# A recurrent attention layer and a gated MLP in one program: the preparation of the MLP's weights is spread differently over the end of the attention part

## The chip, the cores and the metric

One core of a Trainium2 chip runs the whole program. The metric is the device time of one execution in microseconds (us). Before the change three runs gave 663.85, 665.86 and 666.63 us, a median of 665.86 us.

## The reference, cut to what matters

Two parts follow each other. The first is a recurrence over 768 tokens for 4 x 8 pairs of batch and head, each with a state of 40 x 40:

```
for t in range(S):                                   # S = 768
    y[t]  = r[t] @ state
    Sa    = state @ a[t]
    state = state * w[t] - outer(Sa, b[t]) + outer(v[t], k[t])
```

Its output, laid out as x (4 batches x 768 tokens x 320 features), goes through a gated MLP:

```
h = gelu(x @ w_in)                       # 320 -> 1024
u, v = h[..., :512], h[..., 512:]
v_n = layer_norm(v) * g_ln
v_s = w_sg @ v_n + b_sg                  # over the 768 tokens
out = x + (u * v_s) @ w_out              # 512 -> 320
```

"First layer" below is w_in, "last layer" is w_out.

## The kernel before, in words

**Attention.** The 768 tokens are cut into 12 chunks of 64. A chunk is worked off in two halves (`half`, line 488), and each half takes two of the four batches through a chain: `chain1` (PE writes ru, ACT copies it to rhsb), `chain_t` (a transpose of the state, copied to s), `chain2` (PE multiplies by the inverse xt, ACT writes vu), `chain3` (PE writes sp, DVE adds it to the state sc, ACT copies sc to vs; ut and vut), and, for the batches of the half before, `chain4` (PE writes pq, DVE masks it into pqs) and `chain5` (PE writes yp, DVE scales it into yt, SP stores yt to xd in DRAM). The inverse xt of a chunk comes out of a long run of small steps, most of them on GpSimd (tg, x), and then of `inv_back`, `inv_g` and `inv_x` (x1z, gp, gs, xp, and ACT's copies into xt).

**MLP.** In front of its products the weights are prepared. They come as 64-bit floats, and `split64` (line 680) turns a piece into a high and a low 32-bit part in six steps: `load` (SP starts a DMA of the raw piece into a buffer stg), `size` (ACT: sc<-stg), `fields` (DVE: two operations on sc), `scale` (DVE: lt<-stg, stg<-stg,sc, sc<-stg), `parts` (ACT: lt<-lt, and the cast wih<-stg or woh<-stg), `low` (three operations on GpSimd, or on DVE for some pieces of the first layer: lt, stg, and wil or wol). The first layer has 12 pieces of 128 x 256 (`weights_in`), called k0 to k11 below; the last layer has four of 128 x 256 and four of 128 x 64 (`weights_out`), called o0 to o3 and s0 to s3. A raw large piece is 256 KB. The buffers stg are a ring of three (`stage`, line 658) that all pieces share in the order in which they are loaded, so a load waits until the piece three loads back has gone through `low`.

**What sets the order.** Every instruction keeps program order on its engine (`InOrder`, line 105), and SP starts all DMAs of this part of the program in one order. The order is written as numbers: a chunk is 28 positions long, a half 14, and chunk c begins at 28c. `side` (line 886) lists the steps of every weight piece with a position, `half` sorts them among the chain's steps, whose positions are in CH, and calls them in turn. For a first-layer piece `DEC` gives the position of `fields` and whether `low` is on DVE (0) or GpSimd (1), and `DSTEP` the distances of the six steps from it; `DECO` and `DSTEPO` do the same for the last layer, whose `low` is always on GpSimd. So a load is a place in SP's queue, and `size` is a place in ACT's queue; neither knows of the other but by the transfer that `size` waits for.

In SP's queue a half ends with four stores of yt (xd<-yt), two loads of rt and one of vut (`load_rv`), and the next begins with a load of vs; at position 294 there is also `load_x`, four loads of xt from xd. Once the attention part is over, positions go on with `in_v` (three products hv at 338, 342 and 345.87) and the last two batches' chain4 and chain5, then the MLP's main loop (`run`) follows.

Of the kernel before, what the change touches and what calls it, by code (L numbers as in the profile page):

```python
# [53 lines left out]
G1 = 0.044715  # L54
ENDS = {(9, 1): (("g", 0.01),), (10, 1): (("r", 0.01),), (11, 0): (("i", 5.0),)}
PIN = 266.02
DSTEP = ((-9.0, -1.0, 0.0, 0.7, 1.4, 2.4), (-9.0, -1.0, 0.0, 0.7, 1.4, 3.0))
DEC = ((275.0, 0), (280.0, 0), (285.0, 0), (289.66, 0), (295.0, 1), (300.0, 0), (305.0, 1), (310.0, 1), (315.0, 1),
    (320.0, 1), (325.0, 1), (330.0, 1))
PX = 294.02  # L60
# [9 lines left out]
REST = 8  # L70
SGS = (5, 3, 5, 6, 7, 8, 8, 11, 10, 11, 12, 11)
PO = 313.2
DECO = (332.0, 334.0, 336.0, 338.5, 340.5, 342.5, 344.5, 347.0)
DSTEPO = (-4.0, -1.0, 0.0, 0.7, 1.4, 2.4)
SGE = "GVGVGVGVVVGG"
SECOND = 14.0
# [535 lines left out]
class Mlp:  # L612
# [273 lines left out]
    def side(self, c, hf):  # L886

        def at(p, f):
            plan.append((p, f))

        plan = []
        if self.plan is None:
# [4 lines left out]
            def step(k, i):  # L897
                if i == 0:
                    steps[k] = self.weights_in()[k](self.G if DEC[k][1] else self.V)
                steps[k][i]()  # L900

            for k in range(12):
                for i, d in enumerate(DSTEP[DEC[k][1]]):
                    at(max(PIN + 0.1, DEC[k][0] + d), lambda k=k, i=i: step(k, i))
# [7 lines left out]

            for k, p in enumerate(DECO):
                for i, d in enumerate(DSTEPO):
# [171 lines left out]
```

## Time and profile before

| | |
|---|---|
| median of three runs | 665.86 us |
| the profiled execution | 665.51 us, of which its span is 663.8 us |
| PE / DVE / ACT / POOL busy | 87% / 77% / 59% / 58% of the span |
| mean granted TensorE clock | 0.90 of full speed |
| chain that ended last | PE 50%, DVE 24%, ACT 14%, issue 7%, DMA 3% |
| stretch of the weight pieces' `size` on ACT | 326.2 to 415.6 us from the span's start |
| PE busy in the slices of 16.6 us from 398 us and from 431 us | 2 and 6 tenths |

How to read it: a profile row gives the start in us from the span's start, the duration, the engine, the operation, the tile written and the tiles read, a count where rows were merged, and in square brackets how long the engine had been idle and what ended that. SPq rows are DMAs being started, not moved: the row says when SP was busy with the start. The 1.7 us between the span and the execution's time lie outside of the span.

### The profile page before, as it was taken

How to read it: one execution, taken by the hardware profiler on the slowest of the kernel's cores; microseconds unless marked ns; L12 is line 12 of the kernel's file. 1: busy time of each engine (PE TensorE's matmuls, PEld its weight loads, DVE VectorE, ACT ScalarE, POOL GpSimd, SP SyncE). 2: the span in 40 equal slices, each digit the busy share in tenths (PEclk: the TensorE clock that was granted, in tenths of full speed). 3: DMA queues.
4: the chain of work that ended last, by engine and by line, in shares of the span. 5: the costliest groups of instructions: out<-in, count | busy, mean ns of one | idle time of the engine just before them, and what ended most of it. 6: DMA issues, size and time to landing. Idle time of an engine off the chain costs nothing.

```text
span 663.8 us, 22411 instructions
## 1 busy us (share of the span) xinstructions
PE 580.4 (87%) x8950; PEld 525.7 (79%) x8950; DVE 510.4 (77%) x1097; ACT 391.8 (59%) x1106; POOL 385.9 (58%) x869
## 2 busy tenths in 40 slices
PE   6547998989999899998978692969999999999996
PEld 5436787878888778887967682859999999999995
DVE  7875778989889898898777569788679668667732
ACT  5555687978878788797763744654245335424410
POOL 6588886787877878778782455464332433333321
PEclk8555599999999999999978676789999999999999
DMA  6722233443443433433344332331002002100001
GB/s 223 235 78 78 81 95 104 114 118 102 115 109 107 121 106 108 108 93 101 81 113 119 90 88 73 93 110 47 31 13 91 12 19 68 35 31 1 31 24 41
DMA packets 57617, 56.54 MB, mean 85 GB/s; under 512 B 35936, under 2 KB 47456, under 8 KB 57504
## 3 DMA queue, kind: packets, MB, share of 16 engines
q1 hardware_dynamic: 57504, 55.02, 28.9%
q8 instruction: 72, 1.18, 0.7%
q14 instruction: 41, 0.34, 0.2%
HBM read 47.14 MB, written 7.86 MB: 83 GB/s over the span
## 4 chain that ended last, share of the span: by engine, by line
PE 50%; DVE 24%; ACT 14%; issue 7%; DMA 3%; POOL 1%; SPq 1%; DVEq 0%; POOLq 0%; ACTq 0%
PE sg L115 14%; PE op L115 7%; PE hu L115 5%; PE hv L115 5%; PE ab L115 4%; DVE at L115 3%; PE pq L115 3%; DVE fixed L115 3%; PE sp L115 2%; PE ru L115 2%; ACT nts L115 2%; DVE ex L115 2%; ACT xt L115 2%; PE yp L115 2%; DVE kb L115 2%
## 5 line engine op out<-in xcount | busy, mean ns | idle before, releaser
L115 POOL TENSOR_TENSOR tg<-x,n 128x126 f32<-128x126 f32 (+21 forms) x348 | 127.9, 368 | 45.6 <-DVE n L115 7.2
L115 POOL TENSOR_TENSOR x<-x,tg 128x126 f32<-128x126 f32 (+21 forms) x348 | 133.4, 383 | 27.3
L115 POOL TENSOR_TENSOR gx<-g,gy 128x384 fp32r<-128x384 f32 x32 | 33.4, 1046 | 84.6 <-ACT gy L115 83.5
L115 PE MATMUL ab<-at,kb 64*64 64x64 f32 x1536 | 44.5, 248 | 30.6 <-DVE kb L115 17.2
L115 PE MATMUL sg<-wsh,vh 128*128 128x384 f32 x192 | 65.4, 340 | 4.3 <-ACT vh L115 4.3
L115 ACT ACTIVATE nts<-ab 32x256 f32<-32x256 f32 x192 | 62.0, 323 | 10.4 <-DVE at L115 8.0
L115 PEld LDWEIGHTS ab<-at,kb 64*64 64x64 f32 x1536 | 35.9, 155 | 40.4 <-ACT junk L115 14.0
L115 PE MATMUL sg<-wsh,vl 128*128 128x384 f32 x192 | 65.5, 341 | 1.9 <-POOL vl L115 1.9
L115 PE MATMUL sg<-wsl,vh 128*128 128x384 f32 x192 | 65.1, 339 | 0.0
L115 PE MATMUL pq<-rt,vut 128*128 128x128 f32 x384 | 60.5, 306 | 3.8 <-ACT vut L115 3.0
L115 PE MATMUL yp<-pqs,kbt 128*64 128x64 f32 x768 | 50.2, 236 | 14.6 <-DVE pqs L115 13.1
L115 ACT CAST gy<-g 128x384 fp32r<-128x384 f32 x32 | 16.4, 514 | 74.5 <-DVE g L115 74.5
L115 PEld LDWEIGHTS pq<-rt,vut 128*128 128x128 f32 x384 | 52.3, 211 | 7.0 <-ACT vut L115 3.1
L115 PEld LDWEIGHTS yp<-pqs,kbt 128*64 128x64 f32 x768 | 40.7, 147 | 18.0 <-DVE pqs L115 13.7
L115 ACT COPY vs<-sc 64x160 f32<-64x160 f32 x88 | 28.3, 321 | 38.6 <-DVE sc L115 37.7
L115 ACT CAST vh<-v 128x512 fp32r<-128x512 f32 x24 | 14.9, 621 | 55.2 <-DVE v L115 55.2
L115 PE MATMUL yp<-rt,s 80*40 80x64 f32 x704 | 46.4, 232 | 0.0
L115 DVE SCALAR_TENSOR_TENSOR g<-sg,gl,bt 128x384 f32<-128x384 f32 x32 | 19.7, 616 | 32.2 <-PE sg L115 28.4
L115 POOL TENSOR_TENSOR vl<-v,vh 128x512 fp32r<-128x512 f32 x24 | 31.3, 1305 | 22.7 <-ACT vh L115 22.7
L115 DVE TENSOR_TENSOR at<-ab,mask 64x256 f32<-64x256 f32 x96 | 35.9, 409 | 7.6 <-PE ab L115 7.3
L115 PE MATMUL ru<-rhsb,xt 64*64 64x40 f32 x768 | 32.3, 242 | 9.9 <-ACT xt L115 9.9
L115 POOL TENSOR_TENSOR rs<-rs,mhalf 128x1 f32<-128x1 f32 x24 | 13.4, 560 | 46.8 <-DVE rs L115 41.8
(135 smaller groups left out, 1658.9 us busy)
## 6 DMA issues: line engine op xcount, KB each, us to landing
main<-main SPq DMA_DIRECT2D x88, 160.8 KB
vu<-vs SPq DMA_DIRECT2D x24, 160.0 KB
vs<-vb SPq DMA_DIRECT2D x24, 160.0 KB
rt<-rt SPq DMA_DIRECT2D x48, 80.0 KB
vut<-vt SPq DMA_DIRECT2D x24, 160.0 KB
xd<-yt SPq DMA_DIRECT2D x96, 40.0 KB
xt<-xd SPq DMA_DIRECT2D x16, 192.0 KB
out<-y SPq DMA_DIRECT2D x16, 192.0 KB
```

The lines of the kernel that those rows point to most:

```text
L115: return self.tc.keep_in_program_order(f(*a, **k))
```

## The change

Two tables of numbers change. The first-layer pieces' loads stand four positions ahead of `fields` in place of nine; everything else of these pieces keeps its position. The four large pieces of the last layer move from 332 to 338.5 to the gaps of the first layer's last four pieces, and the four small pieces are set 4 and 3 positions apart.

```
-DSTEP = ((-9.0, -1.0, 0.0, 0.7, 1.4, 2.4), (-9.0, -1.0, 0.0, 0.7, 1.4, 3.0))
+DSTEP = ((-4.0, -1.0, 0.0, 0.7, 1.4, 2.4), (-4.0, -1.0, 0.0, 0.7, 1.4, 3.0))
 DEC = ((275.0, 0), (280.0, 0), (285.0, 0), (289.66, 0), (295.0, 1), (300.0, 0), (305.0, 1), (310.0, 1), (315.0, 1),
     (320.0, 1), (325.0, 1), (330.0, 1))
...
-DECO = (332.0, 334.0, 336.0, 338.5, 340.5, 342.5, 344.5, 347.0)
+DECO = (317.5, 322.5, 327.5, 332.5, 336.0, 340.0, 344.0, 347.0)
 DSTEPO = (-4.0, -1.0, 0.0, 0.7, 1.4, 2.4)
```

The first place is SP's queue around position 268, in chunk 9. Before, k0 (stg_6819) stands a half ahead of the others; k1 (stg_6844) and k2 (stg_6892) follow the vs load:

```order
L115 DMA vs0_113<-vb 64x640
L115 DMA stg_6819<-w_in 128x512
L115 DMA vu0_131<-vs 64x640
L115 DMA xd_60<-yt_6682 40x4x64 x2
L115 DMA xd_60<-yt_6790 40x4x64 x2
L115 DMA rt1_125<-rt 40x2x256 x2
L115 DMA vut1_130<-vt 80x8x64
L115 DMA vs1_114<-vb 64x640
L115 DMA stg_6844<-w_in 128x512
L115 DMA stg_6892<-w2 128x512
```

Now, in the same place:

```order
L115 DMA vs0_113<-vb 64x640
L115 DMA vu0_131<-vs 64x640
L115 DMA xd_60<-yt_6682 40x4x64 x2
L115 DMA xd_60<-yt_6790 40x4x64 x2
L115 DMA rt1_125<-rt 40x2x256 x2
L115 DMA vut1_130<-vt 80x8x64
L115 DMA vs1_114<-vb 64x640
L115 DMA stg_6842<-w_in 128x512
L115 DMA stg_6890<-w_in 128x512
```

k0 is now stg_6842 and stands behind the stores, rt, vut and vs, where k1 stood; k1 (stg_6890) takes the place of k2. k2 itself moves to the place that k3 had, behind the next half's vut load.

The second place is SP's queue around position 294, with the loads of xt. Before, k5 (stg_7177) had been loaded ahead of these, and k6 (stg_7290) and k7 (stg_7337) follow the vs load:

```order
L115 DMA stg_7126<-w_in 128x512
L115 DMA stg_7177<-w2 128x512
L115 DMA vu0_131<-vs 64x640
L115 DMA xd_60<-yt_7221 40x4x64 x2
L115 DMA xd_60<-yt_7242 40x4x64 x2
L115 DMA rt1_125<-rt 40x2x256 x2
L115 DMA vut1_130<-vt 80x8x64
L115 DMA xt0_7265<-xd_60 128x384 x2
L115 DMA xt0_7265<-xd_60 64x384 x2
L115 DMA vs1_114<-vb 64x640
L115 DMA stg_7290<-w_in 128x512
L115 DMA stg_7337<-w_in 128x512
```

Now the two loads ahead are those of k3 (stg_7120) and k4 (stg_7175):

```order
L115 DMA stg_7120<-w_in 128x512
L115 DMA stg_7175<-w_in 128x512
L115 DMA vu0_131<-vs 64x640
L115 DMA xd_60<-yt_7219 40x4x64 x2
L115 DMA xd_60<-yt_7240 40x4x64 x2
L115 DMA rt1_125<-rt 40x2x256 x2
L115 DMA vut1_130<-vt 80x8x64
L115 DMA xt0_7263<-xd_60 128x384 x2
L115 DMA xt0_7263<-xd_60 64x384 x2
L115 DMA vs1_114<-vb 64x640
L115 DMA stg_7288<-w2 128x512
L115 DMA stg_7335<-w_in 128x512
```

k5 (stg_7288) has moved behind the stores, rt, vut, the four xt loads and vs, into the place that k6 had; k6 (stg_7335) is right behind it.

The third place is ACT's queue in the last chunk, from position 314 on. Before, k8 (stg_7466), k9 (stg_7526) and k10 (stg_7622) follow each other among the chain's copies:

```order
L115 ACTIVATE sc_7604<-stg_7466 128x256
L115 ACTIVATE vu0_131<-ru_7510 64x2x80 x2
L115 COPY vut0_129<-ut_7624 80x4x64
L115 ACTIVATE lt_7608<-lt_7608 128x256
L115 CAST wih_6815<-stg_7466 128x256
L115 CAST xh_7267<-xt0_7265 128x384 x3
L115 ACTIVATE sc_7648<-stg_7526 128x256
L115 COPY vut0_129<-ut_7652 80x4x64
L115 ACTIVATE lt_7658<-lt_7658 128x256
L115 CAST wih_6815<-stg_7526 128x256
```

Now:

```order
L115 CAST wih_6815<-stg_7524 128x256
L115 ACTIVATE sc_7632<-stg_7602 128x256
L115 ACTIVATE lt_7639<-lt_7639 128x256
L115 CAST woh_7590<-stg_7602 128x256
L115 CAST xh_7265<-xt0_7263 128x384 x3
L115 ACTIVATE sc_7660<-stg_7622 128x256
L115 COPY vut0_129<-ut_7667 80x4x64
L115 ACTIVATE lt_7673<-lt_7673 128x256
L115 CAST wih_6815<-stg_7622 128x256
L115 ACTIVATE sc_7702<-stg_7643 128x256
```

Between k8 (stg_7524) and k9 (stg_7622) stand the three ACT steps of o0 (stg_7602), and o1 (stg_7643) follows k9; DVE and GpSimd have the same pattern. PE's order is the same as before throughout.

## The prediction

> **What bounds the kernel now.** The time by stretches comes first: busy time of each engine, the granted PE clock, the DMA share and GB/s.
>
> ```profile
> 320.00:340.00 20.00, 16.03 (x441) 14.59 (x440) 15.85 (x35) 14.03 (x40) 16.24 (x44) 1.00 0.43 114
> 340.00:350.00 10.00, 9.76 (x131) 8.77 (x128) 8.08 (x21) 4.32 (x12) 8.48 (x20) 0.50 0.31 93
> 360.00:370.00 10.00, 5.32 (x162) 4.71 (x158) 4.08 (x13) 5.93 (x16) 1.22 (x2) 1.00 0.47 126
> 370.00:380.00 10.00, 6.96 (x76) 6.20 (x78) 5.89 (x14) 6.95 (x21) 5.46 (x8) 0.54 0.30 86
> 380.00:390.00 10.00, 10.00 (x126) 9.54 (x122) 4.83 (x15) 4.21 (x13) 3.99 (x6) 0.50 0.37 103
> 400.00:410.00 10.00, 2.83 (x40) 2.41 (x38) 8.87 (x21) 4.53 (x13) 5.57 (x8) 0.74 0.28 81
> 410.00:420.00 10.00, 4.32 (x40) 4.16 (x40) 9.37 (x27) 4.22 (x13) 6.64 (x16) 0.50 0.08 18
> ```
>
> No engine is the bound throughout. From 380 to 390 us PE is full, at half its clock, and DVE, ACT and POOL are idle for half of the time. From 400 to 420 us it is the other way round: PE works 7 us of 20 and DVE 18. Before that, from 360 to 380 us, nobody is busy: engines wait for each other. The waits of PE, by its timeline, say for whom:
>
> ```profile
> 339.03 0.31 PE L115 MATMUL ru<-rhsb,xt 64*64 64x40 f32 x2 [3.67 <-ACT xt L115]
> 372.87 0.43 PE L115 MATMUL ru<-rhsb,xt 64*64 64x40 f32 x2 [4.58 <-ACT xt L115]
> 405.44 0.48 PE L115 MATMUL yp<-pqs,kbt 128*64 128x64 f32 x4 [4.58 <-DVE pqs L115]
> 415.68 0.48 PE L115 MATMUL yp<-pqs,kbt 128*64 128x64 f32 x4 [8.27 <-DVE pqs L115]
> 417.59 1.33 PE L115 MATMUL hu<-xh,wih 128*128 128x384 f32 x3
> ```
>
> The first two wait for ACT's copies of the inverse, the next two for DVE's mask; hu is the first product that needs the first layer's other half. On ACT and DVE the weight pieces stand in the way: their steps are in the same queues, in fixed order. ACT's own timeline shows where k0, k2, k5 and k6 are sized:
>
> ```profile
> 326.06 0.29 ACT L115 COPY s<-tp 80x160 f32<-80x160 f32 x1
> 326.25 0.44 ACT L115 ACTIVATE sc<-stg 128x256 f32<-128x256 f32 x1
> 330.06 0.66 ACT L115 COPY vs<-sc 64x160 f32<-64x160 f32 x2 [3.09 <-DVE sc L115]
> 338.08 0.44 ACT L115 ACTIVATE sc<-stg 128x256 f32<-128x256 f32 x1
> 338.42 0.56 ACT L115 COPY xt<-xp 32x512 f32<-32x512 f32 x1
> 353.71 0.43 ACT L115 ACTIVATE sc<-stg 128x256 f32<-128x256 f32 x1
> 354.66 1.25 ACT L115 ACTIVATE vu<-ru 64x160 f32<-64x160 f32 x4 [0.52 <-PE ru L115]
> 358.58 0.28 ACT L115 COPY s<-tp 80x160 f32<-80x160 f32 x1
> 363.88 0.43 ACT L115 ACTIVATE sc<-stg 128x256 f32<-128x256 f32 x1 [5.01 <-DMA stg<-w_in]
> 364.33 0.66 ACT L115 COPY vs<-sc 64x160 f32<-64x160 f32 x2
> ```
>
> 326.25, 338.08 and 353.71 are k0, k2 and k5, with no wait for a transfer; 363.88 is k6, and ACT stood 5.01 us for its landing. So a late load is seen as a hole in ACT, and 9 us later in PE (372.87).
>
> **The earlier place was worth something: what the later one costs.** SP's timeline shows when a place in its queue is reached:
>
> ```profile
> 312.70 0.54 SPq L115 DMA_DIRECT2D stg<-w_in  x1
> 323.46 1.78 SPq L115 DMA_DIRECT2D xd<-yt  x4
> 327.15 0.62 SPq L115 DMA_DIRECT2D vut<-vt  x1
> 328.54 0.54 SPq L115 DMA_DIRECT2D stg<-w_in  x1
> 337.62 0.62 SPq L115 DMA_DIRECT2D stg<-w_in  x1
> 355.20 3.09 SPq L115 DMA_DIRECT2D xt<-xd  x4
> 358.98 1.06 SPq L115 DMA_DIRECT2D stg<-w_in  x2
> 390.36 0.36 SPq L115 DMA_DIRECT2D stg<-w_out  x1
> 394.85 0.33 SPq L115 DMA_DIRECT2D stg<-w_out  x1
> 399.84 1.64 SPq L115 DMA_DIRECT2D xt<-xd  x3
> 401.52 2.60 SPq L115 DMA_DIRECT2D stg<-w_out  x2
> ```
>
> Four positions look like 4 us, but SP runs behind ACT after each half: the stores wait for yt, and stores, rt, vut and vs take it from 323.46 to 328.44. A load placed there is started when ACT is already at the size step. How long a landing takes is bounded by these rows of ACT:
>
> ```profile
> 393.45 0.43 ACT L115 ACTIVATE sc<-stg 128x256 f32<-128x256 f32 x1 [0.67 <-DMA stg<-w_out]
> 397.85 0.43 ACT L115 ACTIVATE sc<-stg 128x256 f32<-128x256 f32 x1 [3.18 <-POOL wol L115]
> 403.66 0.26 ACT L115 ACTIVATE sc<-stg 128x64 f32<-128x64 f32 x1 [1.75 <-DMA stg<-w_out]
> ```
>
> o1, 256 KB, started at 390.36 and used at 393.45: 3.1 us. o2, started at 394.85, was used at 397.85: 3.0 us (the row names wol, but that had ended and the buffer had been refilled since). A small piece: 403.66 - 401.52 = 2.1 us, a lower end. k6, behind the xt loads: 363.88 - 358.98 = 4.9 us, the upper end. I take 3.1 us where the queue ahead is short and 4.9 us behind xt.
>
> *k0.* It leaves the row at 312.70, 13.5 us ahead of its use, and takes the one at 328.54. ACT is free for it at 326.35 (326.06 + 0.29), the data is there at 328.54 + 3.1 = 331.6: a wait of **5.3 us** (4.3 to 7.1 with the ends). Behind it on ACT stand the copies vs, vut and the inverse's gs and xt; behind `fields` on DVE stand the inverse's transpose and the state's sums sp and sc. PE waits for just these at 339.03. The idle time of 3.09 us ahead of vs is no cover: it is a wait for DVE, and DVE is held by the same piece. So all of it reaches PE.
>
> *k1* is started 0.6 us after k0 and used a whole piece later: no cost. *k2* takes the place of k3, 337.62, and lands at 340.7; ACT was ready at 338.08, and both are moved alike by k0's wait, since the stores ahead wait for yt: **2.6 us** (1.6 to 4.4), ahead of the xt copies at 338.42 for which PE waits. From there to 353 us PE is full at half clock and hides the rest; k3 and k4 are loaded in the middle of a half, where SP is not behind.
>
> *k5* takes the place of k6, 358.98, behind the four xt loads. ACT is ready at 353.71. It now stands until 363.88 by the same clock, in place of standing from 358.86 to 363.88 for k6; k6 is started right behind k5 (two in 1.06 us) and has landed when its turn comes. So the wait grows by 358.86 - 353.71 = **5.2 us**: what ACT did in that time (the four vu copies, s, k5's parts) now comes after the landing, and sp, sc, vs, the inverse's gp and xp wait for it. Some of DVE's share can run while ACT waits: 3 us as the low end, 6 as the high one.
>
> *PE's clock.* Two rows of PE frame the work that now waits for k5:
>
> ```profile
> 356.47 0.66 PE L115 MATMUL sp<-vu,kbt 128*64 128x40 f32 x16
> 361.38 1.08 PE L115 MATMUL ru<-vs,at 128*64 128x40 f32 x32
> ```
>
> sp needs vu, which now follows k5's size: 363.88 + 0.43 + 1.25 = 365.6, so PE idles some 9 us in one piece ahead of it. The rows of the stretches show 0.50 after the idle time at 339 for the whole of 340 to 350, and 0.54 and 0.50 from 370 to 390. If the clock falls here too, the 6.0 us of matmuls from sp to the end of ru take twice as long, but part of that runs beside ACT: 0 to 5 us, I take **2**. The Trainium skill, "TensorE: Matmul & The Clock Gate", section "What's actually happening", has the clock back after about 3.4 us of sustained work; by that this term is 1.7 us at most, and the sum 0.3 us lower with its upper end 3.3 us lower. The rows do not agree: the clock stayed at 0.50 for ten busy microseconds from 380 to 390.
>
> *The last stretch.* Three of the four large last-layer pieces leave the time after PE's full stretch. DVE's timeline has what they take there:
>
> ```profile
> 392.01 1.11 DVE L115 TENSOR_SCALAR sc<-sc 128x256 f32<-128x256 f32 x2
> 404.70 0.68 DVE L115 TENSOR_TENSOR pqs<-pq,mask 128x512 f32<-128x512 f32 x1
> 414.95 0.68 DVE L115 TENSOR_TENSOR pqs<-pq,mask 128x512 f32<-128x512 f32 x1
> ```
>
> From o0's fields at 392.01 to the mask at 404.70 are 12.7 us for four pieces, 3.2 each, so 9.5 us for three: the upper end of the gain. It is not to be had in full, for two reasons. First, the pieces are also limited by the ring of three: a load waits for `low` of the piece three back, then 3.1 us, then the steps. ACT's size rows of k8 and o3 show the pace before, and one row of k9 the hole it has in PE's full stretch:
>
> ```profile
> 375.22 0.43 ACT L115 ACTIVATE sc<-stg 128x256 f32<-128x256 f32 x1
> 381.66 0.42 ACT L115 ACTIVATE lt<-lt 128x256 f32<-128x256 int32 x1 [2.50 <-DVE lt L115]
> 401.00 0.43 ACT L115 ACTIVATE sc<-stg 128x256 f32<-128x256 f32 x1
> ```
>
> Seven steps from k8 to o3 in 25.8 us are 3.7 us each, and the ring alone asks for nearly that, so the eight pieces keep ACT and DVE about as long as before; o2's load, now behind rt and vut, lands about 3 us after ACT is ready and holds vu, which PE needs. Second, s1 still stands in SP's queue behind the four xt loads, as s0 did before (399.84 to 401.52), and these wait for the stores of yt; its landing sets the second mask, the one at 414.95 that PE waited 8.27 us for. Lower end 0, and I take **2 us**, near that end, for the second mask is the later one.
>
> *The rest*, the three hv products and the four smaller pieces, keeps its order; where a small piece has moved past a mask by a place, it is 1 us or less of DVE, in these bounds. `ws` loads and the main loop follow the last yt as before and shift with it.
>
> *Sum* against the profiled execution's 665.5 us: 5.3 + 2.6 + 5.2 + 2 - 2 = 13.1, so **678.6 us**. That execution lies 0.3 us below the median of 665.86 and within the three runs. The ends: 4.3 + 1.6 + 3 + 0 - 5 (half of the upper gain; the full one is a rival) = +4, and 7.1 + 4.4 + 6 + 5 - 0 = +22.5: 669.5 to 688. With the price of the Trainium skill, "DMA: Bandwidth & Descriptors", section "Anatomy of one DMA", 2.0 us and bytes at 436 GB/s (measured there for DMAs issued by GpSimd), 256 KB would land in 2.6 us by estimate, and the sum would be 1 us lower; the trace's 3.0 and 3.1 are what is used.
>
> **The rivals.** *Faster: the landings are quick enough.* Place: ACT ahead of k0's, k2's and k5's size. If a landing took 1.5 us, k0 would be there at 330.04, within the hole that ACT has before vs, k2 at 339.1, and k5 would be hidden in the same way; the waits would be small and the gain of the three pieces stays: 665.5 - 9.5 = 656 us. It decides where the landing falls under about 1.5 us; against it, the shortest seen, of a quarter of the bytes, is 2.1. What speaks for it: DVE does lead the last stretch, and PE's full stretch has room. Chance 0.14.
>
> *No change: both happen in full.* The waits cost 13 to 15 us and the last stretch gives back 9.5 to 12.7, as the ring and SP's queue bind less there than I hold: 662.5 to 669, at 666. For it speaks that ACT has holes in PE's full stretch, like the 2.50 us at 381.66, in which a late load costs nothing. Chance 0.13.
>
> *Worse: the interleaved pieces stall the chain too.* If o1's, k10's and o2's loads, each waiting for a `low` that has just been issued, hold ACT 3 us each in the last chunk and PE has no work ahead, another 6 to 9 us come on top: 685 to 690. Chance 0.07. The waits without compensation, the forecast, keep 0.66.
>
> **How the numbers follow.** Of 665.86 us, 0.5% is 3.3 us, about what a measurement of this kernel can tell from no change: 662.5 to 669.2 is the same. The forecast and the worse case lie above, 0.73; the faster case below, 0.14. The range from 662 to 688 holds the forecast's own, 669.5 to 688, and the no-change case; it leaves out the faster case and most of the worse one, 0.2.
>
> **What the profile after would show.** k0's size row on ACT waits about 5 us for stg<-w_in, with SP starting it at 328.5; k2's waits 2 to 3; k5's waits about 10, and k6's no longer waits. PE's wait for xt at 339 ends 7 to 8 us later, the one at 373 some 13 to 16 us later. In the last stretch the first mask comes a little earlier against the shifted clock and the second hardly. I am wrong if k0's row shows no wait; right in the waits and wrong in the sum if the time from PE's second wait for xt to the first hu product, 417.59 - 372.87 = 44.7 us before, shrinks by more than 5.

## The result, and the profile after

The changed kernel takes 684.11 us (median of four runs, 682.25 to 686.65), the kernel before 666.25 us beside it (four runs, 663.85 to 667.49): 1.0277 times the time, 95% interval 1.0238 to 1.0316, or 17.9 us. The profiled execution took 685.42 us, its span is 683.7 us and its mean granted clock 0.887 (0.900 before).

On the page, the chain that ended last has more than twice the share of DMA that it had (7% for 3%):

```profile
PE 48%; DVE 23%; ACT 13%; DMA 7%; issue 6%; SPq 2%; POOL 1%; DVEq 0%; POOLq 0%; ACTq 0%
```

ACT's timeline shows where. The rows are the copy ahead of k0's size, then the size rows of k0, k2, k5, k6, k7 and s1; in brackets how long ACT stood and for what:

```profile
327.31 0.29 ACT L115 COPY s<-tp 80x160 f32<-80x160 f32 x1
...
333.36 0.43 ACT L115 ACTIVATE sc<-stg 128x256 f32<-128x256 f32 x1 [5.76 <-DMA stg<-w_in]
...
349.38 0.43 ACT L115 ACTIVATE sc<-stg 128x256 f32<-128x256 f32 x1 [3.93 <-DMA stg<-w]
...
373.16 0.43 ACT L115 ACTIVATE sc<-stg 128x256 f32<-128x256 f32 x1 [8.25 <-DMA stg<-w]
...
375.89 0.45 ACT L115 ACTIVATE sc<-stg 128x256 f32<-128x256 f32 x1
...
385.73 0.44 ACT L115 ACTIVATE sc<-stg 128x256 f32<-128x256 f32 x1 [1.81 <-DMA stg<-w_in]
...
424.42 0.26 ACT L115 ACTIVATE sc<-stg 128x64 f32<-128x64 f32 x1 [4.17 <-DMA stg<-w_out]
```

k0, k2 and k5, which had no wait before, now have 5.76, 3.93 and 8.25 us; k6, which had 5.01, has none; k7, which had none, has 1.81 us, just ahead of ACT's next copies of xt; and far behind them stands a new wait of 4.17 us for the small piece s1. SP's timeline has the reason, the place of each load in its queue:

```profile
324.75 1.73 SPq L115 DMA_DIRECT2D xd<-yt  x4
...
329.77 1.00 SPq L115 DMA_DIRECT2D stg<-w_in  x2
...
345.72 0.63 SPq L115 DMA_DIRECT2D stg<-w  x1
...
365.76 3.06 SPq L115 DMA_DIRECT2D xt<-xd  x4
...
369.50 0.58 SPq L115 DMA_DIRECT2D stg<-w  x1
370.13 0.43 SPq L115 DMA_DIRECT2D stg<-w_in  x1
...
382.59 0.37 SPq L115 DMA_DIRECT2D stg<-w_in  x1
...
417.93 1.56 SPq L115 DMA_DIRECT2D xd<-yt  x4
...
419.98 2.05 SPq L115 DMA_DIRECT2D xt<-xd  x4
422.08 1.53 SPq L115 DMA_DIRECT2D stg<-w_out  x3
```

k0 is started at 329.77, behind the stores of yt that began at 324.75; k5 at 369.50, behind the xt loads; k7 at 382.59, among the next half's stores; s1 at 422.08, behind the last but one half's stores and the other xt loads. From start to use are 333.36 - 329.77 = 3.6 us for k0, 3.7 for k2 and 3.7 for k5. PE's timeline shows what came of it:

```profile
350.33 0.43 PE L115 MATMUL ru<-rhsb,xt 64*64 64x40 f32 x2 [7.50 <-ACT xt L115]
...
364.06 1.13 PE L115 MATMUL ru<-rhsb,xt 64*64 64x40 f32 x32
...
373.96 1.40 PE L115 MATMUL sp<-vu,kbt 128*64 128x40 f32 x16 [7.32 <-ACT vu L115]
...
388.53 0.31 PE L115 MATMUL ru<-rhsb,xt 64*64 64x40 f32 x2 [1.75 <-ACT xt L115]
...
433.61 0.48 PE L115 MATMUL yp<-pqs,kbt 128*64 128x64 f32 x4 [8.52 <-DVE pqs L115]
...
435.51 1.33 PE L115 MATMUL hu<-xh,wih 128*128 128x384 f32 x3
```

The first wait for xt, which ended at 339.03, ends at 350.33; the second goes from 372.87 to 388.53; the first hu product from 417.59 to 435.51. DVE's timeline around the two masks completes it:

```profile
417.49 0.74 DVE L115 TENSOR_TENSOR yt<-yp,ex 128x256 f32<-128x256 f32 x2
...
420.96 0.69 DVE L115 TENSOR_TENSOR pqs<-pq,mask 128x512 f32<-128x512 f32 x1
424.71 0.42 DVE L115 TENSOR_SCALAR sc<-sc 128x64 f32<-128x64 f32 x2 [3.07 <-ACT sc L115]
...
432.87 0.68 DVE L115 TENSOR_TENSOR pqs<-pq,mask 128x512 f32<-128x512 f32 x1
```

From the first mask to the second are 11.9 us, where there were 414.95 - 404.70 = 10.25. All rows can be put into three stretches: A, from the copy s ahead of k0's size to PE's second wait for xt; B, from there to the first hu product; C, from there to the end of the span. The same cut serves for all runs below.

| kernel | A | B | C | median, us | ratio to before, 95% interval |
|---|---|---|---|---|---|
| before | 46.8 | 44.7 | 246.2 | 666.25 | |
| after | 61.2 | 47.0 | 248.2 | 684.11 | 1.0277 (1.0238 to 1.0316) |
| e1 loads late, pieces as before | 61.9 | 45.5 | 247.4 | 682.30 | 1.0247 (1.0202 to 1.0292) |
| e2 pieces interleaved, loads early | 46.2 | 46.9 | 247.2 | 668.46 | 1.0032 (1.0005 to 1.0059) |
| e3 after, k0 k2 k5 early | 45.7 | 46.5 | 247.4 | 667.74 | 1.0046 (1.0022 to 1.0071) |
| e4 after, k1 k3 k4 early | 64.3 | 46.9 | 247.5 | 685.47 | 1.0276 (1.0234 to 1.0318) |
| e5 after, s1 early | 62.7 | 43.6 | 247.5 | 680.05 | 1.0215 (1.0164 to 1.0265) |
| e6 before, k6 earlier | 44.0 | 44.8 | 246.5 | 664.02 | 0.9966 (0.9937 to 0.9994) |
| e7 before, k0 late | 53.3 | 43.9 | 246.8 | 671.74 | 1.0080 (1.0046 to 1.0114) |
| e8 before, k5 late | 50.7 | 42.9 | 246.3 | 670.03 | 1.0062 (1.0029 to 1.0095) |
| e9 before, k2 late | 48.6 | 45.4 | 247.9 | 668.41 | 1.0031 (1.0012 to 1.0050) |
| e10 all loads early, interleaved | 44.0 | 43.5 | 247.0 | 664.43 | 0.9969 (0.9950 to 0.9988) |
| e11 before, less work on o0 to o3 | 45.0 | 41.3 | 247.5 | 662.53 | 0.9966 (0.9939 to 0.9993) |
| e12 e10 with o2 later | 44.0 | 44.5 | 247.8 | 664.28 | 0.9981 (0.9959 to 1.0004) |

The kernel before took between 665.3 and 666.4 us (medians) beside these groups of runs. How exact one profile is can be read off the table: C runs over the same order in before, e1 and e6 to e9 and lies between 246.2 and 247.9, and the start of A, ahead of anything that was changed, lies between 324.5 and 328.7 us. So a difference of 1 to 2 us in C or in a span means nothing by itself. Nor does one in A: e11 has the order of the kernel before up to the end of A, and its A is 45.0 where before has 46.8 (k6's landing varies, as e9 shows below). Of the 19.9 us between the two profiled spans, 14.4 came in A, 2.3 in B, 2.0 in C, and 1.25 (327.31 for 326.06) ahead of the change.

### The profile page after: what moved, and what is told of

Read it like the earlier page. It is cut to its first block, busy times and chain, and to the rows that moved or that the text cites. A ratio compares the mean times of both kernels' runs of the same rounds, so it can differ in the third digit from the quotient of the medians.

```text
span 683.7 us, 22405 instructions
## 1 busy us (share of the span) xinstructions
PE 585.5 (86%) x8950; PEld 529.7 (77%) x8950; DVE 511.2 (75%) x1097; ACT 392.3 (57%) x1106; POOL 387.0 (57%) x869
## 4 chain that ended last, share of the span: by engine, by line
PE 48%; DVE 23%; ACT 13%; DMA 7%; issue 6%; SPq 2%; POOL 1%; DVEq 0%; POOLq 0%; ACTq 0%
PE sg L115 14%; PE hu L115 6%; PE op L115 6%; PE hv L115 6%; PE ab L115 4%; DVE at L115 3%; PE sp L115 3%; DVE fixed L115 2%; SPq L115 2%; PE pq L115 2%; ACT nts L115 2%; DVE ex L115 2%; PE yp L115 2%; ACT xt L115 2%; DVE kb L115 2%
## 5 line engine op out<-in xcount | busy, mean ns | idle before, releaser
L115 PE MATMUL yp<-pqs,kbt 128*64 128x64 f32 x768 | 52.5, 242 | 12.3 <-DVE pqs L115 10.0
L115 ACT CAST gy<-g 128x384 fp32r<-128x384 f32 x32 | 16.4, 514 | 74.8 <-DVE g L115 74.8
L115 PEld LDWEIGHTS yp<-pqs,kbt 128*64 128x64 f32 x768 | 42.5, 153 | 15.7 <-DVE pqs L115 10.4
L115 PE MATMUL yp<-rt,s 80*40 80x64 f32 x704 | 48.7, 239 | 0.0
L115 POOL TENSOR_TENSOR rs<-rs,mhalf 128x1 f32<-128x1 f32 x24 | 13.5, 562 | 51.4 <-DVE rs L115 50.3
L115 PE MATMUL sp<-vu,kbt 128*64 128x40 f32 x704 | 35.0, 243 | 8.0 <-ACT vu L115 7.5
```

What stands on the lines that cost most here:

```text
L115: return self.tc.keep_in_program_order(f(*a, **k))
```

## The experiments

**Which half of the change?** e1 has only the loads' distance changed, e2 only the order of the last layer's pieces:

```
e1:  -DSTEP = ((-9.0, -1.0, ...
     +DSTEP = ((-4.0, -1.0, ...          (DECO as before)
e2:  +LOADS = (-9.0, -9.0, -9.0, -9.0, -9.0, -9.0, -9.0, -9.0, -4.0, -4.0, -4.0, -4.0)
                     for i, d in enumerate(DSTEP[DEC[k][1]]):
     +                   d = d if i else LOADS[k]      (DECO as after)
```

> The kernel before with one half of the change: the first layer's loads four positions ahead, the last layer's pieces left at 332 to 347. Theory (late loads): k0, k2 and k5 wait on ACT as in the changed kernel (5.8, 3.9 and 8.3 us there), PE's second wait for xt ends 13 to 15 us later than before, and the last stretch stays as it was: 677 to 683 us. Rival (the interleaved last-layer pieces are what costs): 664 to 670 us.

> The changed kernel with the loads of k0 to k7 back at nine positions ahead; those of k8 to k11 stay at four, since the ring of three wouldn't take them earlier beside the interleaved pieces. So it is the other half of the change alone. Theory (late loads): the first part as before, the last stretch as in the changed kernel, from 2 us shorter than before (my sum) to 4 us longer (the changed kernel's trace, 2.3 us up to hu and 2.0 behind it): 664 to 671 us. Rival (interleaved pieces): 678 to 685 us.

e1 took 682.30 us, nearly all of the loss, with ACT's waits of 5.73, 4.42 and 8.48 us at k0, k2 and k5. e2 took 668.46, 0.3% over the kernel before. So the loads make the loss, and the moved pieces bring none of the gain that I had put against it. Two size rows of e2, of k6 and s1, on ACT's timeline:

```profile
364.52 0.43 ACT L116 ACTIVATE sc<-stg 128x256 f32<-128x256 f32 x1 [4.37 <-DMA stg<-w_in]
...
409.36 0.26 ACT L116 ACTIVATE sc<-stg 128x64 f32<-128x64 f32 x1 [3.58 <-DMA stg<-w_out]
```

The wait for s1 comes with the interleaving, whatever the other loads do; B is 46.9, as after.

**Which loads?** e3 and e4 are the changed kernel with three of the six loads of k0 to k5 set back to nine positions:

```
e3:  +LOADS = (-9.0, -4.0, -9.0, -4.0, -4.0, -9.0, -4.0, -4.0, -4.0, -4.0, -4.0, -4.0)
e4:  +LOADS = (-4.0, -9.0, -4.0, -9.0, -9.0, -4.0, -4.0, -4.0, -4.0, -4.0, -4.0, -4.0)
```

> The changed kernel with only k0's, k2's and k5's loads back at nine positions ahead, all others at four. Theory (three loads fall behind a half's stores and loads in SP's queue, the others do not): nearly as if all were back, 666 to 672 us; k6 waits about 5 us as it did before the change. Rival (every load that stands four positions ahead costs its share of the difference): three of eight are back, so about 677 to 680 us.

> The changed kernel with k1's, k3's and k4's loads back at nine positions ahead, and k0, k2 and k5 left at four: the control for the run before. Theory: no gain, 682 to 687 us. Rival (each load costs its share): about 677 to 680 us.

With k0, k2 and k5 early the time is 667.74: 16.4 of the 17.9 us are gone; k6 waited 3.28 us there, where about 5 were expected. With k1, k3 and k4 early it is 685.47: nothing is gained. The lead in positions is the same for all six; it is the place behind a half's stores, rt and vut that costs. (A is 3 us longer in e4 than after, with 6.57 us at k2. In e4's trace the load of k3, early again, stands right ahead of k2's in SP's queue, and k2's took 5.0 us from its start at 345.52 to its use at 350.53. The times of the two kernels overlap.)

**What is each of the three worth?** e7, e8 and e9 are the kernel before with one of them late:

```
e7:  +LOADS = (-4.0, ...)                the others -9.0
e8:  +LOADS = (..., -4.0, ...)           k5 alone
e9:  +LOADS = (..., -4.5, ...)           k2 alone, so that it stays ahead of k3
```

> The kernel before, with k0 alone loaded four positions ahead of its fields, behind the stores, rt, vut and vs. Theory (each late landing at a half's start reaches PE in full): ACT waits 5 to 6 us for k0, and the time is 5 to 7 us longer, 670 to 673. Rival (a hole later in the chain, such as PE's wait for xt at 339 or ACT's wait for k6, takes most of it back): under 3 us longer.

> The kernel before, with k5 alone loaded four positions ahead of its fields, behind the four xt loads. Theory (what ACT had done between k5 and k6 now follows k5's landing): ACT waits 8 to 10 us at k5 and no longer at k6, PE's clock falls to 0.5 of full speed behind its wait for vu, and the time is 5 to 8 us longer, 670 to 673. Rival (only the difference of the two waits counts, 8.3 - 5.0 = 3.3 us, and DVE and PE do the rest beside it): 668 to 669.

> The kernel before, with k2 alone loaded four and a half positions ahead of its fields, behind the next half's stores, rt and vut. Theory (each of the three loads costs its own wait on ACT): ACT waits 2.5 to 4 us at k2 ahead of the xt copies, and the time is 2.5 to 4 us longer, 668 to 670. Rival (the wait is in the shadow of other work as long as k0 is in time, and only the three together cost what the changed kernel lost): within 1 us of before.

e7: 6.0 us over the kernel before. Its timeline at k0's size, k6's size and PE's second wait for xt:

```profile
333.09 0.43 ACT L116 ACTIVATE sc<-stg 128x256 f32<-128x256 f32 x1 [6.91 <-DMA stg<-w_in]
...
370.21 0.43 ACT L116 ACTIVATE sc<-stg 128x256 f32<-128x256 f32 x1 [5.16 <-DMA stg<-w_in]
...
379.21 0.43 PE L116 MATMUL ru<-rhsb,xt 64*64 64x40 f32 x2 [2.51 <-ACT xt L116]
```

The wait at k0 reaches PE in full (A grows by 6.5), and k6's wait is as long as before, since the stores and the xt loads ahead of k6 moved along. e8: 670.03 us, the lower edge of the theory's 670 to 673. Over the kernel before that is 4.2 us, between its 5 to 8 and the rival's 3.3, and the interval of 1.9 to 6.3 us reaches both. At k5's size and at the second xt:

```profile
365.26 0.43 ACT L116 ACTIVATE sc<-stg 128x256 f32<-128x256 f32 x1 [8.75 <-DMA stg<-w]
...
379.48 0.31 PE L116 MATMUL ru<-rhsb,xt 64*64 64x40 f32 x2 [0.38 <-ACT xt L116]
380.08 1.12 PE L116 MATMUL ru<-rhsb,xt 64*64 64x40 f32 x30 [0.29 <-ACT xt L116]
```

PE now stands ahead of sp and hardly for xt: 0.38 us in place of 4.58. The thirty products of ru behind it took 1.12 us where they took 1.93 in the row of e6 below and in the kernel before, and B is 1.8 us shorter, so that a part of the 3.9 us lost in A comes back. PE's clock fits as the reason: the last pq products ahead of the first mask end 23.4 us behind the second xt in e8 and 24.5 in e7, whose B is 0.8 shorter, and 28.0 to 28.1 in before, e6 and e9, with a B of 44.7 to 45.4. No run sets the clock apart. e9: 2.0 us, below the theory's 2.5 and above the rival's 1, with an interval of 0.8 to 3.3 us that reaches both. The size rows of k2 and k6, and the second xt:

```profile
343.61 0.43 ACT L116 ACTIVATE sc<-stg 128x256 f32<-128x256 f32 x1 [3.94 <-DMA stg<-w]
...
367.11 0.45 ACT L116 ACTIVATE sc<-stg 128x256 f32<-128x256 f32 x1 [2.95 <-DMA stg<-w_in]
...
376.12 0.43 PE L116 MATMUL ru<-rhsb,xt 64*64 64x40 f32 x2 [4.59 <-ACT xt L116]
```

ACT stands 3.94 us for k2, as in the changed kernel, and k6's wait is 2.95 where it was 5.01. Only a part of that is k2's doing: ACT came to k6 0.5 us after the start of its load where it came 0.1 us ahead of it before, but the landing itself was shorter. The start of k6's load in e9, and in e11, which has the order of the kernel before here, with k6's size in e11:

```profile
363.62 0.58 SPq L116 DMA_DIRECT2D stg<-w_in  x1
...
359.06 1.06 SPq L115 DMA_DIRECT2D stg<-w_in  x2
...
362.75 0.44 ACT L115 ACTIVATE sc<-stg 128x256 f32<-128x256 f32 x1 [3.15 <-DMA stg<-w_in]
```

From start to use are 367.11 - 363.62 = 3.5 us in e9 and 3.7 in e11, for 4.9 in before. So this landing varies by itself, the trace of before caught a long one, and how much of k2's wait k6's took back is not shown.

The parts of A are best counted from 44.0 us, the A of the three kernels in which no landing holds ACT there (e6, e10 and e12, below). Before stands 2.8 over it with a wait of 5.01 at k6, e2 2.2 with 4.37, e11 1.0 with 3.15: each time 2.2 us of the wait cost nothing and the rest was paid. By that rule k6's wait is 0.75 us of e9's 4.6 and 3.0 of e7's 9.3, which leaves by estimate 3.9 for k2, its whole wait, and 6.3 for k0, of 6.91. k5's wait of 8.75 in e8, in place of k6's, costs 6.7. After stands 17.2 over 44.0: the waits of 5.76, 3.93 and 8.25, with 2.0 off the last as in e8, are 15.9 of it. Most of the remaining 1.3 would be k7's 1.81, which no run tests alone.

**The old wait, and the new one.** e6 moves k6's load ahead of the stores and the xt loads in the kernel before; e5 does the same for s1 in the changed kernel:

```
e6:  +LOADS = (..., -12.0, ...)          k6 alone, the others -9.0
e5:                  for i, d in enumerate(DSTEPO):
     +                   d = -6.8 if (k, i) == (5, 0) else d
```

> The kernel before, with the load of k6 alone moved ahead of the stores, rt, vut and the four xt loads (12 positions ahead of its fields in place of 9). Theory (a load's place in SP's queue decides, and a landing that ACT stands for reaches PE): ACT's wait of 5.0 us at k6 is gone; DVE's state sums end at 362.06 in the trace of before and its next step stood until 364.34, so 2.3 to 3 us of it are to be had: 662.3 to 663 us. Rival (PE's wait for xt has another lower bound close by, or the ring of three holds the earlier load): within 1 us of before.

> The changed kernel, with the load of the small piece s1 ahead of the four stores of yt and the four xt loads in SP's queue (position 333.2 in place of 336). Theory (the changed kernel's last stretch loses because s1's landing holds ACT 4.2 us and with it the second mask): the wait at s1's size is gone, the second mask comes 3 to 4 us earlier, 680 to 681 us. Rival (the mask waits for the sum of the steps of all the pieces on DVE and ACT, s1's landing is only the last to be seen): another wait takes its place and the time stays within 1.5 us of 684.

e6: 664.02 us, 0.34% below the kernel before, with an interval that just leaves 1 out. At k6's size and at the second xt of its timeline:

```profile
357.87 0.44 ACT L116 ACTIVATE sc<-stg 128x256 f32<-128x256 f32 x1
...
369.14 0.43 PE L116 MATMUL ru<-rhsb,xt 64*64 64x40 f32 x2 [4.58 <-ACT xt L116]
369.74 1.93 PE L116 MATMUL ru<-rhsb,xt 64*64 64x40 f32 x30 [0.17 <-ACT xt L116]
```

The 5.0 us wait is gone and A is 2.8 us shorter, as DVE's rows had allowed. In the time it is 1.8 us by the medians; the theory had 2.3 to 3, so the direction is shown and the size is not settled. e5: 680.05 us, as the theory had it, though its interval and that of the changed kernel just overlap. The timeline at s1's size, the two masks and hu:

```profile
418.60 0.25 ACT L115 ACTIVATE sc<-stg 128x64 f32<-128x64 f32 x1
419.42 0.68 DVE L115 TENSOR_TENSOR pqs<-pq,mask 128x512 f32<-128x512 f32 x1
...
428.18 0.68 DVE L115 TENSOR_TENSOR pqs<-pq,mask 128x512 f32<-128x512 f32 x1
...
430.82 1.33 PE L115 MATMUL hu<-xh,wih 128*128 128x384 f32 x3
```

s1 no longer waits, the masks are 8.8 us apart in place of 11.9, and B is 43.6, 3.3 us less than after. The rows of the other kernels agree: the masks are 8.7 to 8.8 us apart in all three with s1 early (e5, e10, e12), and 11.3 to 11.9 in after, e2, e3 and e4. So one load of 64 KB behind four stores and four loads turned the last stretch from a small gain into a loss.

**What was there to gain at all?** e11 is the kernel before with most of DVE's work on o0 to o3 left out:

```
+    def split64(self, h, l, src, n, G, lean=False):      lean for the four large last-layer pieces
         def size():   ...
+            if lean: return
         def fields(): ...
+            if lean: return
         def scale():  ...  (after lt)
+            if lean: return
```

> The kernel before, with part of the work on the four large last-layer pieces left out: size, fields and two of scale's three operations aren't done, so that 0.4 us of ACT and 2 to 2.4 us of DVE are gone from each piece where it stands, and the output is not the reference's. It bounds what moving these pieces out of the last stretch could bring. Theory (PE's products up to 401 us set the first mask nearly as late as the pieces do): the first mask comes 3 to 4 us earlier against PE's second wait for xt, the second follows it, 661 to 663 us. Rival (the upper end of the gain in the prediction, 9.5 us of DVE for three pieces, is on the path): 655 to 658.

662.53 us, inside the theory's 661 to 663, but not by its mechanism. The timeline at the second xt, the first mask, s0's size, the second mask and hu:

```profile
371.77 0.43 PE L115 MATMUL ru<-rhsb,xt 64*64 64x40 f32 x2 [4.59 <-ACT xt L115]
...
396.90 0.68 DVE L115 TENSOR_TENSOR pqs<-pq,mask 128x512 f32<-128x512 f32 x1
...
400.07 0.26 ACT L115 ACTIVATE sc<-stg 128x64 f32<-128x64 f32 x1 [4.08 <-DMA stg<-w_out]
...
410.38 0.68 DVE L115 TENSOR_TENSOR pqs<-pq,mask 128x512 f32<-128x512 f32 x1
...
413.02 1.33 PE L115 MATMUL hu<-xh,wih 128*128 128x384 f32 x3
```

From the second xt to the first mask are 25.1 us, 6.7 less than the 31.8 before. Not all of this is the work left out. PE's last pq products ahead of the mask end 24.5 us behind the second xt, where they ended 28.0 behind it, because PE was faster before the first of these pieces was reached: its pq at 381.07 took 1.16 us, where the one at 383.76 before took 2.08. In e7 these products also end 24.5 us behind the second xt, with all of the work in place, and the first mask comes 409.44 - 379.21 = 30.2 us behind it. So by this comparison the work is 5.1 of the 6.7 us and PE 1.6: the pieces led there, by more than the theory allowed. But the masks are now 13.5 us apart in place of 10.25, since ACT stands 4.08 us for s0, which is loaded behind the stores and the xt loads. B is 3.5 us shorter than before and 2.7 than in e7, and the time 3.1. So with that work not moved but gone, half of the gain was lost again to the next landing.

**A kernel with every load early.** e10 has the pieces interleaved, all loads ahead of the queue, and s1's too; e12 is e10 with o2 a little later, so that its size does not hold the first vu:

```
e10: +LOADS = (-9.0, -9.0, -9.0, -9.0, -9.0, -9.0, -12.0, -9.0, -4.0, -4.0, -4.0, -4.0)   with e5's line
e12: -DECO = (317.5, 322.5, 327.5, 332.5, ...
     +DECO = (317.5, 322.5, 328.7, 332.5, ...
```

> The changed kernel's order of the pieces, with every load ahead of the queue that held it: k0 to k5 and k7 nine positions ahead of fields, k6 twelve, k8 to k11 four, s1 ahead of the stores of yt and of xt. Theory (interleaving gains once no landing holds ACT): from the 668.5 of the interleaved pieces alone, 2 to 3 us for k6 and 3 to 4 for s1, 661.5 to 663.5, below both kernels. Rival (interleaving itself costs, and the loads only repair that): 664 to 667, no better than the kernel before with k6 ahead.

> The kernel with every load ahead of its queue and the pieces interleaved, with o2 set 1.2 positions later, so that its size step on ACT stands behind the first of the two vu copies it held. Theory (the masks wait for DVE's and ACT's chain of eight pieces, not for PE): PE's two waits for vu (3.5 and 1.4 us) fall below 3 us in sum, the first mask does not move, and the time stays within 1 us of 664.4. Rival (vu is on the path): 661 to 662.5.

e10 took 664.43 us, below both kernels and no better than e6: the rival's range. B was 43.5, 1.3 us less than in e6, but it is 44.5 in e12, and the medians show no gain from the interleaving. In e12, PE's two waits for vu on its timeline are

```profile
389.56 0.68 PE L116 MATMUL ut<-ident,vu 64*80 64x64 f32 x4 [1.01 <-ACT vu L116]
...
391.07 0.69 PE L116 MATMUL ut<-ident,vu 64*80 64x64 f32 x4 [0.83 <-ACT vu L116]
```

1.8 us in sum, where e10 had 3.5 and 1.4, and the time stayed at 664.28. The first mask came no earlier (33.1 us behind the second xt, 32.1 in e10), so shortening these waits gained nothing. A new wait of 0.78 us at k11 came with the move, and so the price of vu alone stays open. Stretch A is 44.0 us, within 0.1, in all three kernels in which no landing holds ACT there (e6, e10, e12).

## Why the prediction was right in direction and 5 us short

The direction, the place and the mechanism came out: 684.1 lies in the range, and the forecast case is the one that happened. By its steps:

*k0, 5.3 us:* ACT stood 5.76. SP started it at 329.77, which is the foreseen 328.54 on a clock 1.25 us late; the landing took 3.6 us in place of 3.1. Alone, it is worth 6.0 us (e7).

*k2, 2.6 us:* 3.93. SP reached it a microsecond later than the shift of k0's wait gave, and the landing took 3.7. The term was undersized, within its bounds. PE's first wait for xt moved by 11.3 us, 10.05 without the late start, where 7.9 was said.

*k5, 5.2 us, with 2 us for the clock:* together 14.4 - 10.05 = 4.4 us. The 10 us of wait foreseen at k5 were 8.25, as the landing took 3.7 us and not the 4.9 that k6 had shown; k6's wait went as said. The clock did fall (sp took 1.40 us for 0.66), but the second wait for xt shrank to 1.75, and this pair of terms came out 2.8 too large. Within the 4.4 lies a wait for which the prediction had no term: k7's load, four positions ahead as well, holds ACT for 1.81 us ahead of the xt copies. In e8, where k7 is loaded early, k7 does not wait, and PE waits 0.38 us for xt in place of 1.75.

*PE's clock against the rule:* in the stretch from 350 us the clock was 0.50 with PE busy for 9.5 of 10 us:

```profile
350.00:360.00 10.00, 9.50 (x118) 8.59 (x120) 6.47 (x20) 5.27 (x15) 1.38 (x5) 0.50 0.16 51
```

The ru group that takes 1.9 us at that clock took 1.13 again at 364.06. The Trainium skill, "TensorE: Matmul & The Clock Gate", section "What's actually happening", has the clock back after about 3.4 us of sustained work; this stretch does not agree with it, nor did those of the kernel before.

*First part in sum:* 13.1 + 2 (the last stretch taken out) = 15.1 was said for A, and 14.4 measured. Two errors of over 2 us each cancelled, and the A of before was a long one: counted from e11's 45.0, it is 16.2. That the sum came within a microsecond is luck in part.

*The last stretch, a gain of 2 us:* this is the step that failed, in its sign. B grew by 2.3 us: 4.3 of the 5.5 us between 678.6 and 684.1. The prediction had named the place, "s1 still stands in SP's queue behind the four xt loads", and took it as a bound on the gain, at no worse than zero. It was a loss, since the interleaving made that queue later: the yt product that the stores wait for came 398.08 - 372.87 = 25.2 us behind the second xt before, and 417.49 - 388.53 = 29.0 after, because all eight large pieces now stand ahead of it on DVE. That last reading is argued from the rows; that s1's landing is the price is shown by e5 (3.3 us of B, 4.1 of the time).

*The upper end of the gain, 9.5 us*, summed DVE's time per piece. e11 bounds it, for s0's load where it stands: with most of that work gone for four pieces, B is 2.7 to 3.5 us shorter. That speaks against the rival "no change", which needed it in full.

*The faster rival* fell with its condition: none of the three landings took under 3.6 us, and it needed 1.5.

*The worse rival*, 3 us per interleaved piece: o2 waited 0.96 us and vu 2.3 and 1.4, and e12, with the waits for vu at 1.8 us in sum, was no faster. Its sum of 685 to 690 is near what was measured, but its cause is not what happened.

*Nothing after hu:* C is 2.0 us longer in this profile. Kernels with one order in C differ by 1.7, so most of it may be chance; that is left open. By the medians the change cost 17.9 us where the sum said 13.1, and of these 4.8 us the last stretch has 4.3.

## What to carry to other kernels

How early a load is has to be read in its queue's terms and not in positions of the program: find what stands ahead of it, what those entries wait for, and whether the user's engine gets there first; three loads of six with one and the same lead cost 16 us and the other three nothing. When work is moved out of a stretch, ask which wait is next in line, and price that one too, with its sign open: a landing that is hidden by the work goes bare with it. A late landing costs what it adds to the waits that were there: k5's wait of 8.75 us in e8 took in k6's of 5.01, and A grew by 3.9.

## What was not expected of the hardware

- Start to use of 256 KB through this queue took 3.6 to 3.7 us at three places in the changed kernel, with the xt loads ahead or without, and 3.1 for k7. In before it was 3.0 to 3.1 for o1 and o2 and 4.9 for k6, and for k6 in the same order 3.7 in e11. The prediction's estimate from the Trainium skill, "DMA: Bandwidth & Descriptors", section "Anatomy of one DMA", was 2.6; none of these came so low.
- PE's speed behind a wait does not go by the length of that wait alone. The thirty ru products took 1.62 us behind a wait for xt of 3.67 us (the first one of before) and 1.93 behind one of 3.69 (the first one of e6); 1.93 behind one of 2.51 (e7), where the granted clock had been at 0.50 since 372 us; 1.12 behind one of 0.38 (e8); and in the changed kernel, behind one of 1.75 us, by PE's timeline

```profile
389.13 1.32 PE L115 MATMUL ru<-rhsb,xt 64*64 64x40 f32 x30 [0.29 <-ACT xt L115]
```

  The return of that speed varies too: 9.3 us behind the second xt the pq products took 1.16 us in e11, and in before, in the same order, still 1.91 us at 15.2 us behind it.
- The start of the same code varied by 4 us from one profile to another (324.5 to 328.7 us at the copy ahead of k0), more than several of the effects that were looked for; cutting the span at rows that both traces have took that out.
